# A first attention batch regrouped by pairs, and the next batch's keys and values loaded ahead of its queries

## The chip, the cores and the metric

The kernel runs on one core of one Trainium2 chip. The core's engines are TensorE (PE, matrix products), VectorE (DVE), ScalarE (ACT), GpSimd (POOL) and SyncE (SP). PE writes its results to PSUM; DVE and ACT bring them from there to SBUF. DMAs are issued here by SP and POOL, two by ACT. The metric is the device time of one launch in microseconds (us), as the median of several runs.

## The reference

Inputs are q, k, v of shape (8 batches, 8 heads, 1024 positions, 64), E and F of shape (64, 1024), w_in (512, 2048) and w_out (2048, 512), all float32. The output has shape (8192, 512).

```python
k_proj = np.einsum('ks,bhsd->bhkd', E, k)
v_proj = np.einsum('ks,bhsd->bhkd', F, v)
scores = np.matmul(q, k_proj.transpose(0, 1, 3, 2)) / np.sqrt(64)
attn = softmax(scores)  # over the 64 projected keys; written out there
x = np.matmul(attn, v_proj)  # then heads side by side: (8192, 512)
h = x @ w_in
out = (h * np.clip(h + 3.0, 0.0, 6.0) / 6.0) @ w_out
```

## The kernel before

Everything runs in bf16 on PE; POOL's loads turn float32 into bf16 on the way.

**Tiling.** A batch has 1024 positions, in two blocks of 512 (t = 0, 1). Heads go in four pairs (j = 0 to 3). The two-layer network takes a block at a time. Its first product gives 16 tiles (fo) of 128 x 512, each from four matmuls of 512 columns (`first_group`, lines 405 to 408). `h_out` (400 to 403) then has ACT make `r` and DVE make `g` from a tile. Its second product gives four row tiles (c), each from 16 matmuls (`second_group`, 414 to 432), copied out of PSUM and sent to DRAM by SP. `second_group` is a generator that stops after every four matmuls, so that several rows, or other work, can be interleaved.

**PSUM.** There are two pools of four banks: `mm` for the network (and for parts of batch 0), `at` for attention.

**Attention of batches 1 to 7** (class `Attention`, lines 169 to 253) is laid between the network's groups of the batch before it. `steps` is a generator; each `next` runs it to its next `yield`. It projects k and v (16 matmuls), copies the keys and values out of PSUM (two DVE copies each), turns the keys by a DMA transpose on SP (`kT`, line 194), then issues the loads of the batch after it on POOL, behind a one-element copy `mark` that waits for `kT`. Then it follows a plan of scores (of two pairs at a time, each with two exps on ACT) and values. `normalised` (222 to 229) sums the exps by a product with ones, multiplies by the values, takes the reciprocal as exp(-ln) on ACT and multiplies on DVE. A number in a plan says how many `yield`s come before its step. The query transpose of a whole batch (`q_transposed`, 148 to 153) is a second DMA transpose on SP.

**Batch 0** (class `First`, lines 260 to 392) is made by hand. In `first_block` (331 to 372) each pair's keys are projected, transposed on PE, multiplied with the queries of block 0, and so on; `busy(n)` (81 to 84) puts n matmuls of ones between, whose result is not used. Block 1's queries, scores and values (`queries`, `second_scores`, `second_values`) come in the network's work of block 0.

**The order of the loads** on POOL's queue is written out in lines 103 to 129: k and half of q of batch 0 by pairs, v by pairs, w_in in parts of 256, 256, 512 and 512 columns, the second half of batch 0's q, the last part of w_in, w_out in quarters, then q, k, v of batch 1.

**The order of the work** is the order of the program on each engine: PE, DVE, ACT, POOL and SP each take their instructions in turn, and a waiting one holds those behind it. Lines 445 to 488 write out batch 0's network with the rest of its attention and all of batch 1's. Lines 491 to 513 are the loop over the other batches: a network group, one step of the next batch's attention, and after every fourth group one row tile of the block before.

Of the kernel before, what the change touches and what calls it, by code (L numbers as in the profile page):

```python
# [9 lines left out]
bf16 = mybir.dt.bfloat16  # L10
# [5 lines left out]
def kernel(  # L16
# [91 lines left out]
    for j in range(KO):  # L108
        load_pair("v", j)

    def load_kqv(b):
        kqv[b] = {}
        for n in ("q", "k", "v"):
            kqv[b][n] = raw_tile(n)
            nc.gpsimd.dma_start(out=kqv[b][n], in_=kqv_dram[n][b])

# [2 lines left out]
    def load_w_in(lo, n):  # L119
        nc.gpsimd.dma_start(out=w_in_sb[:, :, lo:lo + n], in_=w_in_v[:, :, lo:lo + n])  # L120

    for lo, n in ((0, 256), (256, 256), (512, 512), (1024, 512)):
        load_w_in(lo, n)
    load_q0(1, slice(0, H))
    load_w_in(1536, 512)
    for i in range(SB):
        c = slice(i * FO // SB, (i + 1) * FO // SB)
        nc.gpsimd.dma_start(out=w_out_sb[:, c, :], in_=w_out_v[:, c, :])
    load_kqv(1)


    e_t = consts.tile([P, SO, KP], bf16, name="e_t")
# [36 lines left out]
    class Attention:  # L169
        def __init__(self, b, xT):  # L170
            self.b, self.xT = b, xT
            self.kp = att.tile([KP, H, 2, D], bf16, tag="kp", name="kp")
            self.kT = att.tile([P, H, KP], bf16, tag="kT", name="kT")
            self.vp = att.tile([P, H, D], bf16, tag="vp", name="vp")
            self.qT, self.aT = {}, {}


        def project(self, ps):
# [6 lines left out]
        def keys_out(self, ps):  # L185
            for a in range(2):
                nc.vector.tensor_copy(self.kp[:, :, a, :], ps[:KP].rearrange("p (h d) -> p h d", d=D))  # L187

        def values_out(self, ps):
            for a in range(2):  # L190
                nc.vector.tensor_copy(self.vp[a * KP:(a + 1) * KP], ps[KP:].rearrange("p (h d) -> p h d", d=D))  # L191

        def keys_transposed_dma(self):
            nc.sync.dma_start_transpose(self.kT, self.kp.rearrange("p h a d -> p (h a d)"))


        def scores(self, j, alloc):
            self.aT[j] = att.tile([P, 2, 2, HT], bf16, tag="aT", name="aT", bufs=KO + 1)
            tiles = [alloc() for _ in range(2)]
            for a in range(2):  # L200
                for t in range(NB):
                    for r in range(2):
                        nc.tensor.matmul(tiles[r][t * KP:(t + 1) * KP, a * HT:(a + 1) * HT],  # L203
                                         self.kT[r * D:(r + 1) * D, 2 * j + a, :],
                                         self.qT[j][r * D:(r + 1) * D, a, t * HT:(t + 1) * HT],
                                         start=True, stop=True)
# [15 lines left out]
        def normalised(self, j):  # L222
# [4 lines left out]
            for t in range(NB):  # L227
                nc.vector.tensor_mul(self.xT[:, j, t, :], av[t], inverse(lns[t]))  # L228
                yield


        def steps(self, plan):
            ps = pat()
            self.project(ps)
            yield
            self.keys_out(ps)
            self.values_out(ps)
            yield
            self.keys_transposed_dma()
            if self.b + 1 < B:  # L240

                mark = att.tile([1, 1], bf16, tag="mark", name="mark")
                nc.gpsimd.tensor_copy(mark, self.kT[:1, 0, :1])  # L243
                load_kqv(self.b + 1)
            self.qT = {j: qT_dma[self.b][:, j] for j in range(KO)}
            for wait, what, j in plan:
                for _ in range(wait):
                    yield
                if what == "scores":
                    self.scores(j, pat)  # L250
                    self.scores(j + 1, pat)
                else:
                    yield from self.normalised(j)

    LATER = ((6, "scores", 0), (3, "values", 0), (1, "values", 1),
             (1, "scores", 2), (3, "values", 2), (1, "values", 3))

    class First:  # L260
# [70 lines left out]
        def first_block(self):  # L331
            recs = {}

            def scores(j):
                aT = att.tile([P, 2, HT], bf16, tag="aT0", name="aT0", bufs=KO)
                tiles = [pmm() for _ in range(2)]
                self.scores(0, j, tiles, 0)
                for r in range(2):
                    nc.scalar.activation(aT[:, r], tiles[r][:, :HT], AF.Exp, scale=scale)  # L339
                self.aT[0, j] = aT  # L340

            def sums(j):
                ln = log(self.sums(0, j, pmm))
                recs[j] = opool.tile([P, TOK], f32, tag="o_sb", name="o_sb")
                nc.scalar.activation(recs[j], ln, AF.Exp, scale=-1.0)  # L345

            def products(j):
                nc.vector.tensor_mul(self.xT[:, j, 0, :], self.values(0, j, pat), recs[j])

            for j in range(KO):  # L350
                self.keys(j)
                self.queries(0, (j,))
                if j > 0:
                    sums(j - 1)
                self.keys_transposed(j)
                busy(1)
                scores(j)
                if j == 0:
                    busy(2)
            self.vals(0, nc.vector.tensor_copy)  # L360
            busy(1)
            sums(KO - 1)
            self.vals(1, nc.vector.tensor_copy)
            products(0)
            busy(1)
            self.vals(2, nc.scalar.copy)
            products(1)
            busy(1)
            self.vals(3, nc.scalar.copy)
            products(2)  # L370
            busy(1)
            products(3)


# [66 lines left out]
    def g_tile():  # L441
# [2 lines left out]

    xT = x_tile()
    first = First(xT)
    first.first_block()
    x_next = x_tile()
    ahead = Attention(1, x_next).steps(((0, "scores", 0), (3, "scores", 2), (3, "values", 0),
                                        (0, "values", 1), (0, "values", 2), (0, "values", 3)))  # L450
    g = [g_tile(), g_tile()]
    early = [pmm(), pmm()]
    for kos in (range(KO - 1), range(KO - 1, KO)):
        for fo in range(2):
            h_part(early[fo], xT, 0, fo, kos)
    for fo in range(2):
        h_out(early[fo], g[0], fo)
    for fo in range(2, FO):
        first_group(xT, 0, g[0], fo)
        if fo in (9, 10):  # L460
            first.queries(1, (0, 1) if fo == 9 else (2, 3))
        elif fo == 13:
# [24 lines left out]
    whole(ahead)  # L487
    xT = x_next

# [54 lines left out]
```

## Time and profile before

| | us |
|---|---|
| median of 7 runs | 525.32 (524.2 to 526.12) |
| the profiled execution | 525.93 |
| its span, first to last instruction | 524.1 |
| PE, first product (line 397), 1024 matmuls | 238.6 busy |
| PE, second product (line 417), 1024 matmuls | 231.3 busy |
| ACT, r (line 402), 256 x 604 ns | 151.9 busy |
| DVE, g (line 403), 256 x 686 ns | 172.7 busy |
| first matmul of line 397 | at 21.97 |

How to read it: the span is from the first to the last instruction, and the rest of an execution lies around it. Busy times of one engine can be added; those of different engines overlap. PE's matmuls overlap each other, so a matmul of 512 columns has a duration of about 380 ns and yet the next starts about 216 ns later. A number in brackets after an instruction, as in `[3.68 <-DMA kT<-kp]`, is how long the engine sat idle before it and what ended that.

### The profile page before, as it was taken

How to read it: one execution, taken by the hardware profiler on the slowest of the kernel's cores; microseconds unless marked ns; L12 is line 12 of the kernel's file. 1: busy time of each engine (PE TensorE's matmuls, PEld its weight loads, DVE VectorE, ACT ScalarE, POOL GpSimd, SP SyncE). 2: the span in 40 equal slices, each digit the busy share in tenths (PEclk: the TensorE clock that was granted, in tenths of full speed). 3: DMA queues.
4: the chain of work that ended last, by engine and by line, in shares of the span. 5: the costliest groups of instructions: out<-in, count | busy, mean ns of one | idle time of the engine just before them, and what ended most of it. 6: DMA issues, size and time to landing. Idle time of an engine off the chain costs nothing.

```text
span 524.1 us, 7230 instructions
## 1 busy us (share of the span) xinstructions
PE 510.4 (97%) x2808; PEld 224.4 (43%) x2808; DVE 238.1 (45%) x376; ACT 281.8 (54%) x518; POOL 36.5 (7%) x55
## 2 busy tenths in 40 slices
PE   8999979899999999999999999999999999999996
PEld 3444424344444444444444444444444444444442
DVE  2574523664553552554454454535435544444420
ACT  4575335496546763576436664467635765444431
POOL 8410020020020000200002000200000000000000
PEclk9999979999999999999999999999999999999999
DMA  9999969499129811595018941299111110111112
GB/s 171 203 205 219 187 101 219 122 154 185 45 56 200 175 45 40 92 218 123 27 40 144 185 99 40 53 189 184 48 41 31 41 41 20 41 41 42 40 41 80
DMA packets 73155, 55.39 MB, mean 106 GB/s; under 512 B 34464, under 2 KB 64928, under 8 KB 73120
## 3 DMA queue, kind: packets, MB, share of 16 engines
q0 software_dynamic: 30896, 29.36, 35.5%
q1 hardware_dynamic: 42000, 25.17, 18.6%
q10 hardware_dynamic: 224, 0.39, 0.3%
q8 instruction: 22, 0.36, 0.3%
q14 instruction: 13, 0.11, 0.1%
HBM read 59.24 MB, written 16.78 MB: 145 GB/s over the span
## 4 chain that ended last, share of the span: by engine, by line
PE 93%; ACT 3%; DVE 2%; DMA 1%; issue 1%; SPq 0%; DVEq 0%; ACTq 0%
PE mm L417 42%; PE mm L397 42%; PE at L217 3%; PE at L181 3%; PE at L203 2%; DMA ef_f<-in_F_dram 1%; ACT ln L159 1%; ACT r L402 1%; DMA kT<-kp 0%; DVE g L403 0%; ACT o_sb L345 0%; PE mm L84 0%; DVE xT L228 0%; PE at L319 0%; ACT aT L339 0%
## 5 line engine op out<-in xcount | busy, mean ns | idle before, releaser
L403 DVE SCALAR_TENSOR_TENSOR g<-r,mm 128x512 bf16<-128x512 f32 x256 | 172.7, 686 | 222.2 <-ACT r L402 221.8
L397 PE MATMUL mm<-xT,w_in_sb 128*128 128x512 bf16 x1024 | 238.6, 382 | 1.9 <-DVE g L403 1.3
L417 PE MATMUL mm<-w_out_sb,g 128*128 128x512 bf16 x1024 | 231.3, 379 | 0.0
L402 ACT ACTIVATE r<-mm 128x512 f32<-128x512 f32 x256 | 151.9, 604 | 63.7 <-PE mm L397 61.2
L397 PEld LDWEIGHTS <-w_in_sb 128*128 128x128 bf16 x1024 | 97.6, 98 | 127.5 <-issue 17.8
L417 PEld LDWEIGHTS <-g 128*128 128x128 bf16 x1024 | 99.1, 98 | 120.9 <-issue 3.4
L431 ACT COPY o_sb<-mm 128x512 f32<-128x512 f32 x59 | 34.5, 586 | 150.6 <-PE mm L417 150.6
L228 DVE TENSOR_TENSOR xT<-at,rec 128x512 bf16<-128x512 f32 x56 | 38.1, 685 | 24.6 <-ACT rec L164 24.6
L164 ACT ACTIVATE rec<-ln 128x512 f32<-128x512 f32 x60 | 37.6, 639 | 0.0
L159 ACT ACTIVATE ln<-at 128x512 f32<-128x512 f32 x60 | 33.0, 616 | 4.8 <-PE at L217 4.6
L208 ACT ACTIVATE aT<-at 128x512 bf16<-128x512 f32 x56 | 28.9, 612 | 6.1 <-PE at L203 6.1
L243 POOL COPY mark<-kT 1x1 bf16<-1x1 bf16 x6 | 1.1, 177 | 290.3 <-DMA kT<-kp 290.3
L181 PE MATMUL at<-k,e_t 128*64 128x512 bf16 x56 | 13.6, 382 | 0.0
L181 PE MATMUL at<-v,f_t 128*64 128x512 bf16 x56 | 13.4, 382 | 0.0
L203 PE MATMUL at<-qT,kT 64*64 64x256 bf16 x224 | 9.3, 285 | 3.7 <-DMA kT<-kp 3.7
L217 PE MATMUL at<-aT,vp 64*64 64x512 bf16 x112 | 11.5, 377 | 0.1
L217 PE MATMUL at<-aT,ones 64*64 64x512 bf16 x112 | 11.5, 400 | 0.0
L84 PE MATMUL mm<-ones 128*128 128x512 bf16 x24 | 8.6, 462 | 1.5 <-DVE ones L77 1.5
L191 DVE CAST vp<-at 64x512 bf16<-64x512 f32 x14 | 9.7, 694 | 0.3
L203 PEld LDWEIGHTS <-kT 64*64 64x64 bf16 x224 | 5.3, 109 | 9.8 <-issue 5.5
L187 DVE CAST kp<-at 64x512 bf16<-64x512 f32 x14 | 8.9, 674 | 0.9 <-PE at L181 0.9
L181 PEld LDWEIGHTS <-e_t 128*64 128x64 bf16 x56 | 5.6, 109 | 7.8 <-issue 4.1
(56 smaller groups left out, 107.2 us busy)
## 6 DMA issues: line engine op xcount, KB each, us to landing
out_dram<-o_sb SPq DMA_DIRECT2D x63, 256.0 KB, 2.0
q<-in_q_dram POOLq DMA_DIRECT2D x7, 1024.0 KB, 9.7
k<-in_k_dram POOLq DMA_DIRECT2D x7, 1024.0 KB, 14.7
v<-in_v_dram POOLq DMA_DIRECT2D x7, 1024.0 KB, 19.9
w_out_sb<-in_moe_w_out_dram POOLq DMA_DIRECT2D x4, 512.0 KB, 18.9
w_in_sb<-in_moe_w_in_dram POOLq DMA_DIRECT2D x3, 512.0 KB, 13.5
k<-in_k_dram POOLq DMA_DIRECT2D x4, 256.0 KB, 5.4
v<-in_v_dram POOLq DMA_DIRECT2D x4, 256.0 KB, 7.4
```

What stands on the lines that cost most here:

```text
L159: nc.scalar.activation(ln, den, AF.Ln)
L164: nc.scalar.activation(rec, ln, AF.Exp, scale=-1.0)
L181: nc.tensor.matmul(ps[e * KP:(e + 1) * KP], ef_t[e][:, so, :], kqv[self.b]["kv"[e]][:, :, so, :], start=(so == 0), stop=(so == SO - 1))
L203: nc.tensor.matmul(tiles[r][t * KP:(t + 1) * KP, a * HT:(a + 1) * HT], self.kT[r * D:(r + 1) * D, 2 * j + a, :], self.qT[j][r * D:(r + 1) ...
L208: nc.scalar.activation(self.aT[j][:, r].rearrange("p a n -> p (a n)"), tiles[r], AF.Exp, scale=scale)
L217: nc.tensor.matmul(tiles[t][c:c + D].rearrange("p (r n) -> p r n", r=2), stationary(r, 2 * j + a), self.aT[j][r:r + KP, :, a, :], start=Tr ...
L228: nc.vector.tensor_mul(self.xT[:, j, t, :], av[t], inverse(lns[t]))
L397: nc.tensor.matmul(h_ps, w_in_sb[:, ko, fo * P:(fo + 1) * P], xT[:, ko, t, :], start=(ko == 0), stop=(ko == KO - 1))
L402: nc.scalar.activation(r, h_ps, AF.Relu, bias=0.5, scale=1.0 / 6.0)
L403: nc.vector.scalar_tensor_tensor(g[:, fo, :], r, 1.0, h_ps, op0=ALU.min, op1=ALU.mult)
L417: nc.tensor.matmul(o_ps, g[:, fo, c * P:(c + 1) * P], w_out_sb[:, fo, :], start=(fo == 0), stop=(fo == FO - 1))
L431: (copy or nc.scalar.copy)(o_sb, o_ps)
```

## The change

- **Loads.** w_in's first 256 columns come as two loads of 128; the second half of batch 0's q moves behind the last part of w_in; batches 1 and 2 are loaded in the order k, v, q.
- **First pair loop.** Scores run one pair behind the keys, sums two pairs behind. Of the ten `busy` matmuls in `first_block`, four are left. The third pair's values are copied by DVE instead of ACT. `first_block` becomes a generator: products of the last pair come after the first two matmuls of the network.
- **Network of block 0.** The first two tiles are begun with pairs 0 and 1, then 2, then 3 (`two_groups`). Block 1's queries are transposed after tiles 14 and 15 (before: 9 and 10), its scores after the first quarter of the rows (before: after tile 13), its values after the second and third. Three rows are interleaved by quarters (before: two), so one row is left for block 1 (before: two).
- **Block 1.** Its first two tiles use `two_groups` too. Batch 1's attention begins after tile 7 (before: 11), by a plan of its own. `turn` issues the key transpose and, for batch 1, the query transpose right behind it; `mark` then waits for the query transpose.
- **Batch 2's attention** begins with the eleventh step of batch 1's loop (before: the first), by a plan of its own; the four copies are spread. Batch 2's query transpose is issued after all four rows (before: after the second). Batches 3 to 7 keep their plan, written in another way.

```diff
-    for lo, n in ((0, 256), (256, 256), (512, 512), (1024, 512)):
+    for lo, n in ((0, 128), (128, 128), (256, 256), (512, 512), (1024, 512), (1536, 512)):
         load_w_in(lo, n)
     load_q0(1, slice(0, H))
-    load_w_in(1536, 512)
...
-    load_kqv(1)
+    load_kqv(1, "kvq")
...
+        def turn(self):
             nc.sync.dma_start_transpose(self.kT, self.kp.rearrange("p h a d -> p (h a d)"))
+            if self.b == 1:
+                qT_dma[1] = q_transposed(1)
+            if self.b + 1 < B:
+                mark = att.tile([1, 1], bf16, tag="mark", name="mark")
+                nc.gpsimd.tensor_copy(mark, self.kT[:1, 0, :1] if self.b > 1 else qT_dma[1][:1, 0, 0, :1])
+                load_kqv(self.b + 1, "qkv" if self.b > 1 else "kvq")
...
+        def two_scores(self, j):
+            self.scores(j)
+            self.scores(j + 1)
...
-    LATER = ((6, "scores", 0), (3, "values", 0), (1, "values", 1),
-             (1, "scores", 2), (3, "values", 2), (1, "values", 3))
+            for wait, part, *args in plan:
                 for _ in range(wait):
                     yield
+                yield from getattr(self, part)(*args) or ()
+
+    PLAN = ((0, "project"), (1, "keys_out"), (0, "values_out", 0), (0, "values_out", 1), (1, "turn"),
+            (6, "two_scores", 0), (3, "normalised", 0), (1, "normalised", 1),
+            (1, "two_scores", 2), (3, "normalised", 2), (1, "normalised", 3))
+
+    PLANS = {1: ((0, "project"), (0, "keys_out"), (1, "turn"), (0, "values_out", 0), (2, "values_out", 1),
+                 (1, "two_scores", 0), (3, "two_scores", 2), (1, "normalised", 0),
+                 (0, "normalised", 1), (0, "normalised", 2), (0, "normalised", 3)),
+             2: ((10, "project"), (0, "keys_out"), (1, "turn"), (2, "values_out", 0), (3, "values_out", 1),
+                 (1, "two_scores", 0), (2, "two_scores", 2), (3, "normalised", 0),
+                 (0, "normalised", 1), (1, "normalised", 2), (0, "normalised", 3))}
...
             for j in range(KO):
                 self.keys(j)
+                if j > 1:
+                    sums(j - 2)
                 self.queries(0, (j,))
                 if j > 0:
-                    sums(j - 1)
+                    scores(j - 1)
+                else:
+                    busy(1)
                 self.keys_transposed(j)
-                busy(1)
-                scores(j)
-                if j == 0:
-                    busy(2)
+                if j < 2:
+                    busy(1)
+            scores(KO - 1)
             self.vals(0, nc.vector.tensor_copy)
-            busy(1)
-            sums(KO - 1)
+            sums(KO - 2)
             self.vals(1, nc.vector.tensor_copy)
             products(0)
-            busy(1)
-            self.vals(2, nc.scalar.copy)
+            sums(KO - 1)
+            self.vals(2, nc.vector.tensor_copy)
             products(1)
             busy(1)
+            products(2)
             self.vals(3, nc.scalar.copy)
-            products(2)
-            busy(1)
+            yield
             products(3)
...
-    first.first_block()
+    by_pairs = first.first_block()
+    next(by_pairs)
...
-    early = [pmm(), pmm()]
-    for kos in (range(KO - 1), range(KO - 1, KO)):
+    def two_groups(t, kos, more):
+        tiles = [pmm(), pmm()]
+        for i, (fo, part) in enumerate([(fo, part) for part in kos for fo in range(2)]):
+            h_part(tiles[fo], xT, t, fo, part)
+            if i == 0:
+                more()
         for fo in range(2):
-            h_part(early[fo], xT, 0, fo, kos)
-    for fo in range(2):
-        h_out(early[fo], g[0], fo)
+            h_out(tiles[fo], g[t], fo)
+
+    two_groups(0, ((0, 1), (2,), (3,)), lambda: next(by_pairs, None))
     for fo in range(2, FO):
         first_group(xT, 0, g[0], fo)
-        if fo in (9, 10):
-            first.queries(1, (0, 1) if fo == 9 else (2, 3))
-        elif fo == 13:
-            first.second_scores()
-    first.second_values(0)
+        if fo >= FO - 2:
+            first.queries(1, (0, 1) if fo == FO - 2 else (2, 3))
+    ahead = Attention(1, x_next).steps(PLANS[1])
     rows = [second_group(0, 0, g[0], c) for c in range(SB)]
     for i in range(SB + 1):
-        for c in range(2):
+        for c in range(SB - 1):
             next(rows[c], None)
         if i == 0:
-            first.second_values(2)
-    qT_dma[1] = q_transposed(1)
-    for fo in range(FO):
+            first.second_scores()
+        elif i < 3:
+            first.second_values(2 * i - 2)
+    two_groups(1, ((0, 1), (2, 3)), lambda: None)
+    for fo in range(2, FO):
         first_group(xT, 1, g[1], fo)
-        if fo == 7:
-            whole(rows[2])
+        if fo in (7, 8, 9, 10):
+            next(ahead)
         elif fo == 11:
-            next(ahead)
-            next(rows[3])
-            next(ahead)
             whole(rows[3])
-            next(ahead)
     for c in range(SB):
         for _ in second_group(0, 1, g[1], c, nc.vector.tensor_copy):
             next(ahead, None)
-        if c == 1:
-            qT_dma[2] = q_transposed(2)
+    qT_dma[2] = q_transposed(2)
     whole(ahead)
...
-            ahead = Attention(b + 1, x_next).steps(LATER if b > 1 else (
-                (6, "scores", 0), (5, "scores", 2), (4, "values", 0),
-                (1, "values", 1), (1, "values", 2), (1, "values", 3)))
+            ahead = Attention(b + 1, x_next).steps(PLANS.get(b + 1, PLAN))
```

More of the change, by code (lines that the diff above doesn't have):

```diff
@@ L109, with load_kqv @@
         load_pair("v", j)
-    def load_kqv(b):
+    def load_kqv(b, order="qkv"):
         kqv[b] = {}
-        for n in ("q", "k", "v"):
+        for n in order:
             kqv[b][n] = raw_tile(n)
@@ L174, in __init__, with project @@
             self.vp = att.tile([P, H, D], bf16, tag="vp", name="vp")
-            self.qT, self.aT = {}, {}
-        def project(self, ps):
+            self.aT = {}
+        def project(self):
+            ps = self.ps = pat()
             for so in range(SO):
@@ L183, in project, with keys_out, values_out, scores @@
                                      start=(so == 0), stop=(so == SO - 1))
-        def keys_out(self, ps):
+        def keys_out(self):
             for a in range(2):
[L187 to L197, printed above, removed]
+                nc.vector.tensor_copy(self.kp[:, :, a, :], self.ps[:KP].rearrange("p (h d) -> p h d", d=D))
+        def values_out(self, a):
+            nc.vector.tensor_copy(self.vp[a * KP:(a + 1) * KP], self.ps[KP:].rearrange("p (h d) -> p h d", d=D))
+        def turn(self):
+            nc.sync.dma_start_transpose(self.kT, self.kp.rearrange("p h a d -> p (h a d)"))
+            if self.b == 1:
[4 more added lines that the diff above has]
+                load_kqv(self.b + 1, "qkv" if self.b > 1 else "kvq")
+        def scores(self, j):
+            qT = qT_dma[self.b]
             self.aT[j] = att.tile([P, 2, 2, HT], bf16, tag="aT", name="aT", bufs=KO + 1)
-            tiles = [alloc() for _ in range(2)]
+            tiles = [pat() for _ in range(2)]
             for a in range(2):
@@ L204, in scores @@
                                          self.kT[r * D:(r + 1) * D, 2 * j + a, :],
-                                         self.qT[j][r * D:(r + 1) * D, a, t * HT:(t + 1) * HT],
+                                         qT[r * D:(r + 1) * D, j, a, t * HT:(t + 1) * HT],
                                          start=True, stop=True)
@@ L229, in normalised @@
                 yield
+        def two_scores(self, j):
+            self.scores(j)
+            self.scores(j + 1)
         def steps(self, plan):
[L233 to L246, printed above, removed]
+            for wait, part, *args in plan:
                 for _ in range(wait):
                     yield
[L249 to L253, printed above, removed]
-    LATER = ((6, "scores", 0), (3, "values", 0), (1, "values", 1),
-             (1, "scores", 2), (3, "values", 2), (1, "values", 3))
+                yield from getattr(self, part)(*args) or ()
[8 more added lines that the diff above has]
+                 (0, "normalised", 1), (1, "normalised", 2), (0, "normalised", 3))}
     class First:
@@ L446 @@
     first = First(xT)
-    first.first_block()
+    by_pairs = first.first_block()
+    next(by_pairs)
     x_next = x_tile()
-    ahead = Attention(1, x_next).steps(((0, "scores", 0), (3, "scores", 2), (3, "values", 0),
-                                        (0, "values", 1), (0, "values", 2), (0, "values", 3)))
     g = [g_tile(), g_tile()]
-    early = [pmm(), pmm()]
-    for kos in (range(KO - 1), range(KO - 1, KO)):
+    def two_groups(t, kos, more):
[4 more added lines that the diff above has]
+                more()
         for fo in range(2):
-            h_part(early[fo], xT, 0, fo, kos)
-    for fo in range(2):
-        h_out(early[fo], g[0], fo)
+            h_out(tiles[fo], g[t], fo)
+    two_groups(0, ((0, 1), (2,), (3,)), lambda: next(by_pairs, None))
     for fo in range(2, FO):
         first_group(xT, 0, g[0], fo)
-        if fo in (9, 10):
-            first.queries(1, (0, 1) if fo == 9 else (2, 3))
-        elif fo == 13:
-            first.second_scores()
-    first.second_values(0)
+        if fo >= FO - 2:
+            first.queries(1, (0, 1) if fo == FO - 2 else (2, 3))
+    ahead = Attention(1, x_next).steps(PLANS[1])
     rows = [second_group(0, 0, g[0], c) for c in range(SB)]
     for i in range(SB + 1):
-        for c in range(2):
+        for c in range(SB - 1):
             next(rows[c], None)
         if i == 0:
-            first.second_values(2)
-    qT_dma[1] = q_transposed(1)
-    for fo in range(FO):
+            first.second_scores()
[3 more added lines that the diff above has]
+    for fo in range(2, FO):
         first_group(xT, 1, g[1], fo)
-        if fo == 7:
-            whole(rows[2])
+        if fo in (7, 8, 9, 10):
+            next(ahead)
         elif fo == 11:
-            next(ahead)
-            next(rows[3])
-            next(ahead)
             whole(rows[3])
-            next(ahead)
     for c in range(SB):
```

## The prediction

> **What bounds the kernel now.** I read the page's busy times first, then the busy time by windows, then the order of time on PE, and last SP and DVE around each hole.
>
> ```profile
> PE 510.4 (97%) x2808; PEld 224.4 (43%) x2808; DVE 238.1 (45%) x376; ACT 281.8 (54%) x518; POOL 36.5 (7%) x55
> ...
> PEclk9999979999999999999999999999999999999999
> ```
>
> PE is the bound, and the one low digit of its clock is in the slice from 65.5 to 78.6 us. Windows (columns: length, then busy us and instructions of PE, PEld, DVE, ACT, POOL, then clock, DMA share, GB/s) show where it is short of work:
>
> ```profile
> 66.50:69.53 3.03, 0.38 (x2) 0.00 (x0) 0.00 (x0) 0.58 (x1) 0.00 (x0) 1.00 0.38 111
> 69.53:76.37 6.84, 5.81 (x28) 2.34 (x29) 1.24 (x2) 3.26 (x6) 2.80 (x4) 0.50 0.63 80
> ...
> 145.25:206.49 61.24, 61.24 (x337) 26.71 (x336) 28.67 (x44) 34.69 (x65) 2.80 (x4) 1.00 0.53 106
> ```
>
> The last is one batch of the steady loop. Its content is 256 matmuls at 0.216 us (the 40 from 21.97 take 8.74 us in the chain of waits, 0.2185 each; 16 take 3.45 in the loop), 55.2 us, plus projection 1.85, scores 2 x 0.65, sums and values 4 x 0.65: 61.0 of 61.24. So batches 2 to 7 have nothing to give, and the change leaves their plan as it is. What can be won lies before 135 us. PE in order of time there:
>
> ```profile
> 40.96 0.40 PE L319 MATMUL at<-aT,vp 64*64 64x512 bf16 x2 [0.62 <-DVE xT L392]
> 41.55 0.40 PE L319 MATMUL at<-aT,vp 64*64 64x512 bf16 x2 [0.20 <-DVE xT L392]
> ...
> 70.56 1.07 PE L203 MATMUL at<-qT,kT 64*64 64x256 bf16 x16 [3.68 <-DMA kT<-kp]
> 71.56 5.98 PE L397 MATMUL mm<-xT,w_in_sb 128*128 128x512 bf16 x16
> ...
> 95.96 0.38 PE L397 MATMUL mm<-xT,w_in_sb 128*128 128x512 bf16 x1 [0.64 <-DVE xT L228]
> ...
> 103.91 2.75 PE L397 MATMUL mm<-xT,w_in_sb 128*128 128x512 bf16 x12 [1.29 <-DVE g L403]
> ```
>
> Four holes, and the 16 matmuls after the largest take 5.98 us where 3.6 is usual. Why kT came so late is on SP's queue:
>
> ```profile
> 48.27 13.85 SPq L151 DMA_TRANSPOSE qT<-q  x1
> 62.16 5.69 SPq L432 DMA_DIRECT2D out_dram<-o_sb  x2
> 67.90 1.23 SPq L194 DMA_TRANSPOSE kT<-kp  x1
> ```
>
> SP sat 13.85 us in the issue of batch 1's q transpose, because the 16 DMA engines were full with the loads of k and v; v landed at 61.39 (29.75 + 31.64). kT's transpose waited for v (projection), for an output and for the copies.
>
> **What the Trainium skill says.** "TensorE: Matmul & The Clock Gate", part 1: the clock falls to half after an idle window of about 3.4 us. Here it fell at 69.53, 2.6 us after PE's last matmul ended (66.9), and stayed at half for 6.83 us; the trace agrees in kind and is a little quicker. "PSUM — Partial Sum Buffer", section on engine and sequencer instructions: matmuls start and finish in program order, so one late operand holds all that is behind it. The 3.68 us show it. "DMA: Bandwidth & Descriptors", section on issuing engines: SP's, ACT's and POOL's DMAs share the 16 engines. The same q transpose took 15.9 us to land at 48.27 beside the loads, and 6.7 to 8.5 in the four cases after 160 us where the loads were done. The same page's specifications: below 512 bytes a transfer leaves line rate. No packet of this kind from HBM is in the trace, so I bound it below.
>
> **A. The head (first pair loop and w_in).** In the loop each pair takes 2.29 us (keys at 12.11, 14.41, 16.70), of which ACT works 0.64 + 0.60 + 0.63 = 1.87 and waits 0.4 to 0.5, because exp, sums, log and reciprocal of one pair follow each other:
>
> ```profile
> L159 ACT ACTIVATE ln<-mm 128x512 f32<-128x512 f32 x4 | 2.4, 597 | 2.6 <-PE mm L319 2.6
> ```
>
> With scores one pair and sums two pairs behind, ACT can run through. By hand, with the durations of this trace: exp of pair 0 at 10.4, then ACT is its own bound, the last reciprocal ends near 19.3 instead of 19.6, but the values of pairs 0 to 2 are no longer behind it. v's last quarter lands at 18.09 in both. Six idle matmuls fewer (24 to 18) are 6 x 0.22 on PE where it is dense. PE then reaches the first group at 19.8, puts products(3) (0.33 us) behind two matmuls of it, and would be at tile fo = 4 at 24.0, against 25.43 (21.97 + 4 x 0.866). But tile 4 needs w_in columns 512 to 1023:
>
> ```profile
> L120 POOL DMA_DIRECT2D w_in_sb<-in_moe_w_in_dram x1: 745/745/745, 12.6 to 12.6; - x1
> ...
> DMA to landing us min/median/max: 11.7/11.7/11.7
> ```
>
> They land at 24.26 now. In the change 256 columns come as two loads of 128, 1024 rows of 256 bytes (as written) for 512 rows of 512. Packets of 1024 bytes took 98 ns and of 512 bytes 60 ns. In a line 256 bytes take 41: 1024 x 41 against 512 x 60 over 16 engines that overlap 1.4 times is 0.5 us more. Ends: 0.2 (from the throughput, 203 and 370 packets a us, also in a line) and 1.4 (as dear as 512 bytes, 370 a us). I take 0.35: landing at 24.6, so the head gives 25.43 - 24.65 = **0.75 us** (-0.3 to 0.9), and DMA becomes its bound. The later w_in parts come earlier, since q's second half now stands behind them (about 32.4, needed at 34.3).
>
> **B. Second half of block 0.** The four sums and values at 39.93 take 1.95 us to the next matmul where 0.65 is their size: 1.3 lost, since 8 matmuls (1.7 us) lie between the two second_values while log, reciprocal and product of the first take 3.7. Now three rows interleave, 12 matmuls (2.6 us) lie between, and the scores stand between the first and second step. 2.6 + 0.65 + 0.3 against 3.7: 0.15 remains. **1.15 us** (0.7 to 1.3). ACT's backlog of two r tiles is gone too, as the scores come after the last tile. w_out's quarters land at 34.6, 37.2, 39.7, 42.3, plus 0.35; needed at about 36, 39, 42.5, 46.
>
> **C. Batch 1's keys.** Removed: 3.75 us (4.06 from the last matmul to the scores, less its own 0.22 and a switch of 0.09) and the half clock: scores 1.00 for 0.56, eleven matmuls 4.67 for 2.38, the next 0.07: 2.8. Together **6.55 us**, if nothing is late in its place. The new times, from tile 4 at 24.65: 11 groups to fo = 14 (34.2), queries and fo = 15 to 36.0, four steps of 12 matmuls with scores and two second_values to 48.6, and fo = 7 ends at 55.5. k and v are now first in the queue: 5.03 us for each load when alone (q: 42.28 to 47.31), so 47.7 and 52.7, v perhaps 0.6 later for outputs. POOL issues them long before (its last three loads now go out at 24.55 to 29.75, each held until an earlier one has landed; one issue more shifts this by under 1 us). The projection (55.5 to 57.4) waits for neither. keys_out ends at 59.1 (2 x 0.674); kT's issue 1.2, landing 2.6: 61.7. Behind it on SP is qT(1). q lands near 60: 52.7 + 5.03 + 2.2 for three outputs (128 packets of 95 ns each over 16 engines, 0.75 an output). So qT issues at 60.3 and, with no load in flight (batch 2's wait for the mark, which now reads qT), lands 6.75 to 8.5 later: 67.0 to 68.8. The scores want it after fo = 15, row 3 and four matmuls: 57.4 + 6.93 + 3.45 + 0.86 = 68.7. It fits, by little: each us of qT beyond that is a us of PE. SP's outputs behind qT have four buffers and hide. Batch 2's loads start at 67.7 instead of 71.06, q last: 89.3 by the same 19.85; its transpose, now on SP behind all four rows of block 1 (it stood behind row 1), ends by 97 and is wanted at 103.
>
> **D. Batches 1 and 2.** The last sums of batch 1 come one step earlier: 0.65 + 1.73 + 0.65 = 3.0 us of PE cover a chain of 2.84 (93.08 to 95.92), so the 0.8 at 94.95 (1.02 less 0.22) goes. Batch 2's four copies in a row hold DVE:
>
> ```profile
> 100.43 1.27 DVE L187 CAST kp<-at 64x512 bf16<-64x512 f32 x2
> 101.73 1.40 DVE L191 CAST vp<-at 64x512 bf16<-64x512 f32 x2
> 103.16 3.12 DVE L403 SCALAR_TENSOR_TENSOR g<-r,mm 128x512 bf16<-128x512 f32 x5
> ```
>
> Now two come right behind the projection's 1.85 us, when DVE has run empty, and the others singly; one copy of 0.69 is worked off in four groups (0.866 - 0.69 = 0.18 each). The 1.45 at 102.23 goes. New: the scores of pairs 2 and 3 come two groups after those of 0 and 1. Four exps (2.4 us) must free their PSUM tiles; PE is back after 0.65 + 1.73 = 2.4 and waits perhaps 0.4 (0 to 1). Net **1.85 us** (1 to 2.25). kT(2) lands at 101.3, wanted at about 103.
>
> Sum: 0.75 + 1.15 + 6.55 + 1.85 = 10.3. Span 524.1 - 10.3 = 513.8. The profiled execution took 525.93, 1.8 outside its span, so 515.6 for it; it stands 0.6 above the median 525.32, and from the median it is 515.0.
>
> **The rivals.** 1: qT takes kT's place. q is last in the queue now, and the slack is 0 to 1.7 us. For: the smallest margin of all. Against: SP and the DMA engines are idle then. 2.5 us late gives 517.5; once PE idles 2.6 us the half clock adds 2.8: 520.3. 2: the head gains nothing (256-byte rows at the upper end) and the closer scores in batch 1 cost 1 us more: 10.3 - 1.05 - 1.0 = 8.2, so 517.1 to 518. For: neither is in the trace. Against: ACT is busy 57% of a steady batch. 3, slower: qT(1) meets traffic as it did at 48.27 and 114.32, where it took 15.9 and 16.9 us. From 60.3 it lands at 77.2 and the scores wait 8.5 us, plus 2.8 at half clock: 11.3 for the 6.55 removed, 4.75 against the 3.75 of A, B and D: 526.3. It decides from a landing at 76.2 on. Against: only outputs can be in flight, no load. 4, no change: the holes only move (C's waits 7.5 us again); the same place, a little earlier.
>
> **How the numbers follow.** Forecast 0.70, with its own range 513.3 (all holes gone, 0.9 + 1.3 + 6.55 + 2.25 = 11.0, and spread of the runs) to 517; rival 1 0.12; rival 2 0.11; rival 3 0.05; rival 4 0.02. The range goes to 519, which takes in rival 2 and the milder half of rival 1. About 0.2% (1 us) is what a measurement tells from no change. Faster 0.93, same 0.02, slower 0.05.
>
> **What would show it.** A: the first L397 near 19.8 and tile 4 waiting for DMA w_in near 24.6. B: values of the second pair waiting under 0.3. C: no half clock at 65 to 78 and the scores of batch 1 near 68.7 with under 0.5 of wait; a wait for DMA qT is rival 1. D: no wait over 0.5 for DVE g or xT between 85 and 135. The steady batches must stay at 61.24; if they don't, the prediction is wrong where I looked least.

## The result, and the profile after

The changed kernel takes 518.13 us (median of 12 runs, 517.74 to 519.26), against 524.93 for the kernel before (31 runs, 523.15 to 526.95). The ratio is 0.9871, with a 95% interval from 0.9858 to 0.9883: 6.8 us faster. The forecast was 515.0, with a range of 513.3 to 519: up to 517 for the forecast itself, and from there to 519 for its rivals. The direction holds, and the measured time lies in the part that was added for the rivals; 3.1 us of the gain did not come. In spans it is 524.1 against 516.3, 7.8 us; the profiled execution of before was 1.0 us above its median, that of the changed kernel is at its own (518.07).

The page of the changed kernel, busy times and clock:

```profile
PE 506.5 (98%) x2802; PEld 222.8 (43%) x2802; DVE 239.6 (46%) x377; ACT 282.1 (55%) x517; POOL 37.2 (7%) x56
...
PEclk9999999999999999999999999999999999999999
```

The low digit of the clock is gone. PE has 3.9 us less busy time; by my sum for part C some 2.8 of it were matmuls at half clock. Windows of the changed kernel (length, then busy us and instructions of PE, PEld, DVE, ACT, POOL, clock, DMA share, GB/s):

```profile
48.03:68.20 20.17, 20.17 (x101) 8.87 (x99) 13.20 (x21) 10.96 (x19) 0.66 (x2) 1.00 0.97 195
68.20:86.48 18.28, 17.90 (x126) 7.21 (x126) 7.18 (x12) 12.50 (x24) 2.14 (x3) 1.00 1.08 183
86.48:101.70 15.22, 15.22 (x79) 6.81 (x78) 11.71 (x18) 8.48 (x15) 0.00 (x0) 1.00 0.66 136
101.70:137.40 35.70, 33.90 (x199) 14.14 (x197) 18.18 (x29) 24.02 (x46) 2.82 (x4) 1.00 0.84 140
137.44:198.68 61.24, 61.24 (x338) 26.70 (x336) 28.68 (x44) 34.71 (x65) 2.80 (x4) 1.00 0.54 106
```

Block 1 of batch 0 has no hole any more (a hole is time in which PE has nothing to run) up to batch 1's scores at 68.2, and the steady batch is what it was, 61.24. The 1.8 us in which PE is not busy between 101.70 and 137.40 are in batch 1's loop, where batch 2's attention is laid in. The loop had 2.0 us of them before, but in other places. By stages, with the starts of matmuls read from the timelines:

| stage | before | after | change | forecast |
|---|---|---|---|---|
| start to tile 4 of the first product | 25.43 | 24.42 | -1.0 | -0.75 (A) |
| tile 4 to the start of batch 1's loop | 69.1 | 62.1 | -7.0 | -7.7 (B and C) |
| batch 1's loop | 50.1 | 50.3 | +0.2 | -1.85 (D) |
| the rest | 379.5 | 379.5 | 0 | 0 |

PE in order of time, changed kernel, where the holes of before were and where the new ones are:

```profile
41.62 0.41 PE L321 MATMUL at<-aT,ones 64*64 64x512 bf16 x4
41.86 0.39 PE L321 MATMUL at<-aT,vp 64*64 64x512 bf16 x4
...
68.21 0.63 PE L210 MATMUL at<-qT,kT 64*64 64x256 bf16 x16
...
73.55 0.89 PE L224 MATMUL at<-aT,vp 64*64 64x512 bf16 x4
...
84.40 0.40 PE L224 MATMUL at<-aT,vp 64*64 64x512 bf16 x2 [0.20 <-DVE xT L235]
...
105.46 0.41 PE L210 MATMUL at<-qT,kT 64*64 64x256 bf16 x7 [0.88 <-DVE vp L190]
...
123.67 0.85 PE L224 MATMUL at<-aT,vp 64*64 64x512 bf16 x4
...
131.26 0.40 PE L224 MATMUL at<-aT,vp 64*64 64x512 bf16 x2 [0.85 <-ACT ln L158]
```

The brackets tell only a part of what is lost. Where nothing waits, four sums and four values take 0.57 us from their first start to the next matmul's; here they take 1.38 from 73.00, 1.16 from 83.58, 1.02 from 123.43 and 1.86 from 129.74, so 0.8, 0.6, 0.45 and 1.3 us are lost. The scores at 104.06 lose 1.2 (1.74 for 0.57). Of these only the 0.45 is old: the kernel before loses as much at batch 2's last values:

```profile
133.46 0.85 PE L217 MATMUL at<-aT,vp 64*64 64x512 bf16 x4
```

The second_values of block 0 (line 321) have no bracket now, and batch 1's scores start at 68.21 without a wait. SP's queue shows by how much:

```profile
58.33 1.28 SPq L194 DMA_TRANSPOSE kT<-kp  x1
60.51 4.86 SPq L150 DMA_TRANSPOSE qT<-q  x1
65.42 22.55 SPq L436 DMA_DIRECT2D out_dram<-o_sb  x5
```

kT landed at 61.11 (2.79 after its issue), qT at 67.17 (6.66), 1.0 us before the scores. The two largest new waits are in batch 1's loop. At the first, DVE (changed kernel, order of time):

```profile
102.79 1.88 DVE L407 SCALAR_TENSOR_TENSOR g<-r,mm 128x512 bf16<-128x512 f32 x3
104.71 0.70 DVE L190 CAST vp<-at 64x512 bf16<-64x512 f32 x1
```

The second value copy ends at 105.41, and PE goes on at 105.46. Until that copy the projection's tile holds one of the four PSUM banks of attention, and the two score steps want all four. At the second, ACT:

```profile
124.03 1.08 ACT L158 ACTIVATE ln<-at 128x512 f32<-128x512 f32 x2
128.12 0.59 ACT L435 COPY o_sb<-mm 128x512 f32<-128x512 f32 x1 [3.00 <-PE mm L421]
128.60 0.63 ACT L163 ACTIVATE rec<-ln 128x512 f32<-128x512 f32 x1
129.13 0.59 ACT L406 ACTIVATE r<-mm 128x512 f32<-128x512 f32 x1
129.61 0.63 ACT L163 ACTIVATE rec<-ln 128x512 f32<-128x512 f32 x1
```

Pair 2's logs are done at 125.1, but its reciprocals stand behind the copy of a row, which waits 3.00 us for that row's 16 matmuls. The products that free pair 2's banks come after the reciprocals, the last at 131.15, and pair 3's logs come after the reciprocals too, the first at 131.21. Pair 3's values, which want a free bank, go on at 131.26, 0.05 us after that log. The trace names the log, and the other waits shown here also end 0.05 us after what they wait for; by the order of the tiles one would have expected the product, which ended 0.11 before. Either way it is ACT's order behind the row copy that comes late.

### The profile page after: what moved, and what is told of

It reads as the page before. It is cut to its first block, busy times and chain, and to the rows that moved or that the text cites. A ratio compares the mean times of both kernels' runs of the same rounds, so it can differ in the third digit from the quotient of the medians.

```text
span 516.3 us, 7223 instructions
## 1 busy us (share of the span) xinstructions
PE 506.5 (98%) x2802; PEld 222.8 (43%) x2802; DVE 239.6 (46%) x377; ACT 282.1 (55%) x517; POOL 37.2 (7%) x56
## 4 chain that ended last, share of the span: by engine, by line
PE 91%; DMA 3%; DVE 2%; ACT 1%; POOL 1%; issue 1%; DVEq 0%; ACTq 0%; POOLq 0%
PE mm L421 42%; PE mm L401 42%; PE at L224 3%; PE at L181 3%; DMA w_in_sb<-in_moe_w_in_dram 2%; PE at L210 1%; DMA k<-in_k_dram 1%; DVE g L407 1%; POOL q L97 0%; ACT aT L215 0%; POOL k L101 0%; DVE xT L235 0%; ACT ln L158 0%; DVE vp L190 0%; ACT r L406 0%
## 5 line engine op out<-in xcount | busy, mean ns | idle before, releaser
L401 PE MATMUL mm<-xT,w_in_sb 128*128 128x512 bf16 x1024 | 235.8, 379 | 0.5 <-DMA w_in_sb<-in_moe_w_in_dram 0.5
L401 PEld LDWEIGHTS <-w_in_sb 128*128 128x128 bf16 x1024 | 97.0, 98 | 125.1 <-issue 12.6
L224 PE MATMUL at<-aT,vp 64*64 64x512 bf16 x112 | 12.7, 378 | 1.3 <-ACT ln L158 0.9
L84 PE MATMUL mm<-ones 128*128 128x512 bf16 x18 | 7.0, 519 | 1.5 <-DVE ones L77 1.5
L224 PEld LDWEIGHTS <-ones 64*64 64x64 bf16 x112 | 3.2, 103 | 11.9 <-issue 11.9
```

The source lines that it names most:

```text
L224: nc.tensor.matmul(tiles[t][c:c + D].rearrange("p (r n) -> p r n", r=2), stationary(r, 2 * j + a), self.aT[j][r:r + KP, :, a, :], start=Tr ...
L401: nc.tensor.matmul(h_ps, w_in_sb[:, ko, fo * P:(fo + 1) * P], xT[:, ko, t, :], start=(ko == 0), stop=(ko == KO - 1))
```

## The experiments

Each starts from the changed kernel. Times are medians, to be held against 518.13; the kernel before took 524.6 to 525.2 on the chips of these runs, and the changed kernel 517.90 when it was run again on another chip, so 0.2 us of a difference can be the chip. Tile 4 of the first product starts at 24.17 to 25.03 in eight traces with the changed kernel's head, so a few tenths of a us are read from medians here and not from the span of one trace.

**Batch 1's load order undone.**

```diff
-    load_kqv(1, "kvq")
+    load_kqv(1, "qkv")
```

> Only batch 1's load order goes back to q, k, v. Theory one: keys and values first is what part C rests on. v then lands near 60.5, the projection at 54.7 waits 5.5 to 6 us, the clock falls to half for another 2.8: 526 to 527. Theory two: the place of the projection (tile 7 for 11) and of the q transpose did it, and the order is worth little: under 520.

Measured: 525.23, ratio to before 0.9999 (0.9986 to 1.0013). Without this one line nothing of the change's gain is left. Its PE in order of time, then a window:

```profile
54.96 0.40 PE L181 MATMUL at<-k,e_t 128*64 128x512 bf16 x1
59.77 0.58 PE L181 MATMUL at<-v,f_t 128*64 128x512 bf16 x1 [4.41 <-DMA v<-in_v_dram]
```

```profile
59.19:62.61 3.42, 2.84 (x14) 1.48 (x14) 0.00 (x0) 0.00 (x0) 0.00 (x0) 0.50 0.02 6
```

v landed at 59.73; the projection waited 4.4 us and then ran at half clock for 3.4. Theory one's mechanism holds, and its 526 to 527 was about 1 us too high. The profiled execution (524.15) is one of three at a mean granted clock of 0.997; the other nine are at 0.992 or 0.993 and took 524.8 to 525.7, so 3.4 us at half clock is the short case. The load order goes with the projection's early place at tile 7: in the kernel before v landed at 61.39, and the projection at tile 11 lost only 0.4 us to it (2.26 for 1.85). The new order with the projection left at tile 11 was not tried.

**Batch 2's loads not held back by batch 1's query transpose.**

```diff
-                nc.gpsimd.tensor_copy(mark, self.kT[:1, 0, :1] if self.b > 1 else qT_dma[1][:1, 0, 0, :1])
+                nc.gpsimd.tensor_copy(mark, self.kT[:1, 0, :1])
```

> Batch 2's loads wait for batch 1's key transpose, as in the kernel before, and not for its query transpose. Theory one (rival 3 of the prediction): the query transpose at 60.5 then shares the 16 DMA engines with three loads from about 62 on, lands near 76 as the one at 112.6 does (15.97 us), and the scores of batch 1 wait from 68.2 on for some 8 us, with half clock: 526 to 529. Theory two: a transpose whose packets are queued first is slowed little, as the one at 87.7 of the kernel before (8.67 us beside the end of one load): it lands by 70 and the time is 518 to 520.

Measured: 523.95, ratio to before 0.9987 (0.9977 to 0.9996). SP's queue and PE in that kernel:

```profile
60.00 5.18 SPq L150 DMA_TRANSPOSE qT<-q  x1
```

```profile
72.40 0.63 PE L210 MATMUL at<-qT,kT 64*64 64x256 bf16 x16 [4.02 <-DMA qT<-q]
72.96 4.21 PE L421 MATMUL mm<-w_out_sb,g 128*128 128x512 bf16 x11
```

The transpose landed at 72.27, 12.3 us after its issue, so neither theory had the size: nearly twice the 6.66 it takes alone, less than the 16.9 of my rival. The kind is rival 3's. PE waited 4.0 us, and its clock was at half from 72.95 to 76.37. That `mark` waits for the query transpose is therefore the other half of part C: without it 5.8 of the 6.8 us are lost.

**The first pair loop undone** (idle matmuls and order as before; loads and the rest as changed).

```diff
             for j in range(KO):
                 self.keys(j)
-                if j > 1:
-                    sums(j - 2)
                 self.queries(0, (j,))
                 if j > 0:
-                    scores(j - 1)
-                else:
-                    busy(1)
+                    sums(j - 1)
                 self.keys_transposed(j)
-                if j < 2:
-                    busy(1)
-            scores(KO - 1)
+                busy(1)
+                scores(j)
...
```

> The first pair loop and the tail of block 0's attention go back to the old order with ten idle matmuls; loads and the rest stay. Theory one: the loop's new order is worth what tile 4 shows, 25.43 against 24.41, so 1.0 us: about 519.1, with the first network matmul near 22 and no wait for w_in at tile 4. Theory two: tile 4 is bound by the loads alone and the old loop would meet them there too: within 0.3 of 518.1.

Measured: 518.89, 0.8 slower (six runs, none under 518.78). Its first network matmul is at 21.66 (19.82 in the changed kernel), and it reaches tile 4 at 25.13 without a wait for w_in. Theory one, a little smaller. Tile 4's time alone would show it less well, as the changed head starts it at up to 25.03.

**w_in's third part split.**

```diff
-    for lo, n in ((0, 128), (128, 128), (256, 256), (512, 512), (1024, 512), (1536, 512)):
+    for lo, n in ((0, 128), (128, 128), (256, 256), (512, 256), (768, 256), (1024, 512), (1536, 512)):
```

> w_in's columns 512 to 1023 come as two loads of 256. Tile 4 then needs the first of them, near 23.1 instead of 24.4, and its wait (0.66 us, 0.88 from start to start) goes. Theory one: the head passes it on, 517.5. Theory two: batch 1's v is the next bound, landing at 54.6 where the projection starts at 55.0; brought forward by 0.65 it waits for v, and the time stays at 517.9 to 518.2.

Measured: 517.55 from four runs, 517.35 to 518.25. The changed kernel waits at tile 4:

```profile
24.42 2.76 PE L401 MATMUL mm<-xT,w_in_sb 128*128 128x512 bf16 x12 [0.50 <-DMA w_in_sb<-in_moe_w_in_dram]
```

In this kernel that wait is gone, but its profiled execution, which is the one of 518.25, has a new one at 55.17:

```profile
55.17 0.38 PE L181 MATMUL at<-v,f_t 128*64 128x512 bf16 x1 [0.52 <-DMA v<-in_v_dram]
```

So both theories are seen, the second at least in this execution; how much is kept on average four runs do not settle.

**The first stall of batch 1's loop: value copies earlier.**

```diff
-             2: ((10, "project"), (0, "keys_out"), (1, "turn"), (2, "values_out", 0), (3, "values_out", 1),
-                 (1, "two_scores", 0), (2, "two_scores", 2), (3, "normalised", 0),
+             2: ((10, "project"), (0, "keys_out"), (1, "turn"), (1, "values_out", 0), (2, "values_out", 1),
+                 (3, "two_scores", 0), (2, "two_scores", 2), (3, "normalised", 0),
```

> Batch 2's two value copies come three and one steps earlier in its plan; the scores stay where they are. Theory one: the 1.15 us between the scores' matmuls at 104.3 in the changed kernel is a PSUM bank, which the projection holds until its last value copy, and that copy stands on DVE behind three g tiles. Then the wait ends, the span falls from 516.3 to about 515.2, and the time from 518.1 to about 517.0. Theory two: the two score steps are too close for ACT's exps, and the copy is only the last of several. Then PE waits for ACT in the same place and the time stays within 0.3 us of 518.1.

Measured: 517.32 (four runs, 517.04 to 517.59), 0.8 faster. In its trace the 16 matmuls of the scores run in one piece:

```profile
104.67 0.63 PE L210 MATMUL at<-qT,kT 64*64 64x256 bf16 x16
```

Theory one, the bank. The 1.2 us of this stall are gone from the trace: from tile 4 to the end it is 1.1 us shorter than the changed kernel's. The median shows 0.8 of them.

**Batch 2's old plan and load order.**

```diff
-             2: ((10, "project"), (0, "keys_out"), (1, "turn"), (2, "values_out", 0), (3, "values_out", 1),
...
+             2: ((0, "project"), (1, "keys_out"), (0, "values_out", 0), (0, "values_out", 1), (1, "turn"),
+                 (6, "two_scores", 0), (5, "two_scores", 2), (4, "normalised", 0),
+                 (1, "normalised", 1), (1, "normalised", 2), (1, "normalised", 3))}
...
-                load_kqv(self.b + 1, "qkv" if self.b > 1 else "kvq")
+                load_kqv(self.b + 1, "qkv")
```

> Batch 2's attention goes back to its old plan (projection at the first step, four copies in a row, scores five steps apart) and its loads to the order q, k, v; all else is the changed kernel. My prediction's part D gave the new plan 1.45 us of DVE stall less, at a price of 0.4: then this kernel is about 1 us slower than the changed one, 519.1. The trace of the changed kernel says that the new plan's stalls (1.1 at 104.3, 0.5 at 123.7, 1.0 to 1.3 at 130.0) pay all of it back: then it is faster by about 1 to 1.5 us, 516.6 to 517.1, with the DVE wait of 1.3 us back after the projection.

Measured: 519.03, 0.9 slower. The number is that of the first reading, but not for its reason. PE shows the DVE wait and one that neither reading had:

```profile
89.02 0.38 PE L181 MATMUL at<-v,f_t 128*64 128x512 bf16 x1 [1.44 <-DMA v<-in_v_dram]
```

```profile
96.62 1.24 PE L401 MATMUL mm<-xT,w_in_sb 128*128 128x512 bf16 x5 [1.29 <-DVE g L407]
```

With everything 8 us earlier, batch 2's v lands (88.97) after the old place of the projection. The old plan's four copies cost what they did before, 1.29 us of idle time, and the projection takes 3.65 us where 1.85 is usual, so the late v costs 1.8. The test mixes two things and does not price the plan alone. Less the late v it would be at 517.2, 0.9 faster than the changed kernel; that is an estimate from the trace, and it speaks for the second reading.

**Batch 1's second scores one step earlier.**

```diff
-                 (1, "two_scores", 0), (3, "two_scores", 2), (1, "normalised", 0),
+                 (1, "two_scores", 0), (2, "two_scores", 2), (2, "normalised", 0),
```

> Batch 1's second pair of scores comes one step earlier, so that two steps of the second product lie between its exps and the first sums. Theory one: the 0.54 us lost at 73.0 to 74.0 is four PSUM banks held by exps; it goes, 517.6. Theory two: something else on ACT holds the banks and the loss moves to the scores: 518.0 to 518.2.

Measured: 517.48 (four runs, 516.95 to 517.80). The sums and values at 73.40 take 0.79 us for 1.38, and the scores at 71.01 have no wait. Theory one; the loss there was 0.8 us and not the 0.54 of the expectation, which counted two of its gaps.

**Everything together.** To the split of w_in and the earlier scores comes a plan for batch 2 that puts scores into block 0 of batch 1, where ACT copies no rows, and each pair's sums so that no row copy falls between its log and its reciprocals, but for the first pair.

```diff
-             2: ((10, "project"), (0, "keys_out"), (1, "turn"), (2, "values_out", 0), (3, "values_out", 1),
...
+             2: ((3, "project"), (0, "keys_out"), (1, "turn"), (1, "values_out", 0), (2, "values_out", 1),
+                 (3, "two_scores", 0), (5, "two_scores", 2), (3, "normalised", 0),
+                 (1, "normalised", 1), (2, "normalised", 2), (1, "normalised", 3))}
...
-                load_kqv(self.b + 1, "qkv" if self.b > 1 else "kvq")
+                load_kqv(self.b + 1, "qkv")
```

> The changed kernel with the split of w_in, the earlier second scores of batch 1, and another plan for batch 2 (q, k, v order; projection at the fourth step, scores at steps 11 and 16 where no rows are copied out, sums and values at tiles 2, 5, 9 and 12 of block 1, where the steady batches have them). If the three stalls of batch 1's loop (1.1, 0.5, 1.3 us) come from the plan's places, they all go, and with the other two parts about 3.5 to 4 us: 514.2 to 514.8. If batch 1's loop must pay in any order (ACT and DVE have 0.27 and 0.18 us of room in each tile), the gain is under 2 us.

Measured: 515.10, ratio 0.9808 (0.9789 to 0.9828), a gain of 3.0 where 3.5 to 4 were expected; batch 2's projection still lost 0.8 us waiting for v (2.67 for 1.85). One step later, alone and with the rest, beside the changed kernel on the same chip:

```diff
-             2: ((10, "project"), (0, "keys_out"), (1, "turn"), (2, "values_out", 0), (3, "values_out", 1),
...
+             2: ((4, "project"), (0, "keys_out"), (1, "turn"), (1, "values_out", 0), (2, "values_out", 1),
+                 (3, "two_scores", 0), (4, "two_scores", 2), (3, "normalised", 0),
+                 (1, "normalised", 1), (2, "normalised", 2), (1, "normalised", 3))}
...
-                load_kqv(self.b + 1, "qkv" if self.b > 1 else "kvq")
+                load_kqv(self.b + 1, "qkv")
```

> The changed kernel as it is, on the same chip as the next two, so that differences of about 1 us can be read: 518.1, between 517.7 and 518.7.

> The changed kernel with another plan for batch 2 alone: order q, k, v, projection at the fifth step, where v (landing near 89.6) is there, copies spread, scores at steps 12 and 16, sums and values at tiles 2, 5, 9 and 12 of block 1. If all three stalls of batch 1's loop come from where the plan puts its steps, it is 2.6 to 2.9 us faster than the changed kernel, 515.3; the step of my prediction that failed (part D) would then be a plan that was worse than it could be, and not a limit of the loop. If the loop must pay, under 1.3.

> The best version so far (515.1) with batch 2's projection one step later, so that it no longer waits 0.6 us for v: 514.5.

| kernel | us | ratio to before |
|---|---|---|
| changed kernel again | 517.90 | 0.9871 (0.9848 to 0.9894) |
| with the other plan for batch 2 alone | 515.40 | 0.9822 (0.9798 to 0.9845) |
| with all three | 514.16 | 0.9797 (0.9771 to 0.9823) |

The plan and load order of batch 2 alone are worth 2.5 us. A window over batch 1's loop of the last kernel, and of the changed kernel over a stretch that holds the same stalls:

```profile
84.00:133.60 49.60, 49.60 (x283) 21.51 (x281) 30.19 (x47) 32.98 (x62) 2.82 (x4) 1.00 0.88 152
```

```profile
84.00:136.00 52.00, 50.00 (x281) 21.25 (x280) 31.00 (x48) 34.20 (x63) 2.82 (x4) 1.00 0.83 146
```

PE is busy throughout in the first, and 2.0 us short in the second; 0.2 of the 2.0 are the wait at 84.2, which the last kernel has too, at 83.0, ahead of its window. The new plan moves all of batch 2's steps at once. That the row copy between log and reciprocals made the stall at 130 is thus read from the order of ACT and was not tried alone. This last version beats both kernels, by 3.7 and 10.5 us.

## Why the prediction was right, and where it was off

**A, the head: right.** Tile 4 came at 24.42 (24.65 was forecast) and it does wait for w_in, so the loads are the head's bound. The undone loop gives 0.8 against my 0.75. The 256-byte rows, which I could only bound, took 41 ns a packet, as the straight line had it: with 60 ns for 512 bytes and 98 for 1024 there is no step at 512. w_in's third part landed at 24.37, only 0.1 later than before. Three readings were off without harm. The last quarter of v landed at 19.32 and not at 18.09 as in the kernel before, and PE waited 0.44 us for it; why is open, and w_in hides it. PE by itself would have been at tile 4 at 23.8 and not 24.0. And the 16.70 in my row of key starts belongs to the values; the keys start at 7.58, 10.10, 12.11 and 14.41, still 2.3 apart on average.

**B: right, and a little larger.** No wait is left where I kept 0.15, and the hole had been 1.4 us, not 1.3: I gave the four sums and values 0.65 of their own where 0.57 is enough. It was not undone alone; this is read from the two traces.

**C: the mechanism right, one landing wrong without harm.** kT landed at 61.1 (61.7 forecast), qT at 67.2 (67.0 to 68.8), the scores ran at 68.2 (68.7). v was forecast at 52.7, perhaps 0.6 later, and landed at 54.64; the projection wanted it at 55.03. That the margin of 2 us shrank to 0.4 and still held is luck, and with w_in split, where the projection starts at 54.25, PE did wait for v. The two experiments on C show that it hangs on two things together: v before q (7.1 us without) and no load beside the transpose (5.8 without). Rival 3 was the right mechanism with too high a price: with loads released early the transpose took 12.3 us, not 16.9.

From tile 4 to batch 1's loop -7.7 was forecast and -7.0 came. The removals were larger than forecast: 1.4 for B, 6.55 for C, and 0.4 that batch 1's projection had waited for v at 61 in the kernel before, which no part had; 8.4 in all. What the sum left out is what stands behind the scores: 0.8 us at 73, where PE waits for banks held by exps, since the first sums now come one step behind the second scores and not three, and 0.6 at 84, where it waits for a product. 8.4 - 1.4 is 7.0.

**D: the step that failed.** I had 1.85 us and it gave -0.2. The removals were right: neither the wait for xT at 95 (0.8) nor the one for DVE's g (1.45) is there any more. The term for what is new was 0.4 us, "PE is back after 0.65 + 1.73 = 2.4 and waits perhaps 0.4"; the loop now loses 1.2 at 104, 0.45 at 123.7 and 1.3 at 130, of which the 0.45 is old, so 2.5 is new: 2.25 - 2.5 is about -0.2. I had priced spread copies by DVE's time alone, 0.69 each. A copy that comes later also keeps its source: the projection's PSUM bank lived until the last one, and the test of the bank shows that this was the stall at 104. And I had looked at DVE and at the exps, but not at where the plan's steps fall between the row copies on ACT, which takes its instructions in order and waits in one of them for 16 matmuls. Batch 2's new plan as built was thus worse than its old one, and the part of D that held is batch 1's earlier sums. The plan of the last experiments shows that the loop itself has room: with the same instructions in other places PE has no hole there.

The measured 518.13 lies beside rival 2's 517.1 to 518, by chance. Its half on batch 1's loop had the right place, but half the size (1 us, where D fell short by 2.05) and another reason (how close the scores are); its half on the head was wrong.

**Spans and medians.** The span fell by 7.8 us and the median by 6.8. For 49 executions of the kernel before, run beside the experiments, the mean granted clock is on record, and they fall into three groups: 7 at 0.998 or more took 523.1 to 523.7 us, 28 at 0.995 to 0.997 took 524.3 to 525.6, and 14 at 0.993 took 525.5 to 526.8. The profiled execution, with its 6.83 us at half clock, is of the last kind. By these clocks, how long PE runs at half clock after the same stall differs from execution to execution, and the median pays about half of the 2.8 us that I took for C from one profile (the groups' medians are 523.4, 524.6 and 526.1). The changed kernel's runs are all at 0.998 or more, within 1.5 us. Taking the gain of one execution off a median was a second mistake: of the 3.1 us that did not come, 2.05 are D, 0.7 what stands behind C's scores less the larger removals, 0.6 this, and A gave back 0.25.

## What to carry to other kernels

When a stall is a late transfer, look at what stands ahead of it on all the queues, the loads' own order first: without one changed string, "kvq" for "qkv", nothing of this change's gain was left. A copy out of PSUM that is moved later is not free on account of its engine having time: ask who wants the bank. And of a chain that is split over steps (log, then reciprocal), look at what the other work puts between the two halves on an engine that runs in order. And before a stretch at half clock goes into a sum, look at how much of it the median execution has.

## What the hardware showed

A DMA transpose of 1 MB landed 6.66 us after its issue with no load in flight, 12.3 with three loads released 1.9 us behind it, and 15.97 in the middle of such loads (at 112.58 in the changed kernel).

The clock fell to half 2.65 us after PE's last matmul ended in the kernel before, and 3.8 and 4.6 us after in two experiments (55.36 to 59.19, 68.38 to 72.95); in the last of these PE was already at work again for half a us. It stayed there for 6.83, 3.41 and 3.41 us in these three executions, one length and its double. "TensorE: Matmul & The Clock Gate", part 1, of the Trainium skill gives a window of 3413 ns that runs free of the kernel, which fits the lengths; the delay of 2.65 us is shorter than the page's one idle window.
